# Attention and feed-forward on one core: the first batch's chain moved to PSUM, its inverse slopes spread by TensorE, its order planned anew

## The chip, the cores and the metric

The kernel runs on one core of a Trainium2 chip. The metric is the device time in microseconds, the median of the runs. Before the change it is 1262.75 us (three runs, 1261.84 to 1263.13).

## The reference

Two blocks follow each other: pooled attention (4 batches of 12288 queries, 768 keys each) and a two-layer feed-forward with `h - tanh(h)` in the middle.

```python
def _attn_ref(q, kv, w_sr):          # q: 4 x 12288 x 128, kv: 4 x 384 x 32 x 128
    kv_pool = kv.reshape(B, H // r, r, W // r, r, C).mean(axis=(2, 4))   # r = 4
    kv_flat = kv_pool.reshape(B, -1, C) @ w_sr                           # k = v
    s = scale * (q @ kv_flat.transpose(0, 2, 1))
    a = np.exp(s - s.max(-1, keepdims=True))
    a /= a.sum(-1, keepdims=True) + 1e-09
    return a @ kv_flat

def _moe_ref(x, w_in, w_out):        # w_in: 128 x 2048, w_out: 2048 x 128
    h = x @ w_in
    return (h - np.tanh(h)) @ w_out
```

## The kernel before

The 49152 queries are cut into 96 groups of 512, 24 per batch. A group passes through two stages. *Attention*: three pairs of score matmuls (line 1036), a root on ScalarE (1040), its square on GpSimd (1043), three pairs of value matmuls (1086), and a linear part (1058 to 1076); VectorE joins them into `dl` (1090), GpSimd makes `dr` of it (1093). *Feed-forward*: the function `h - tanh(h)` is expanded about the hidden values at the batch's mean value, so each of eight pairs of "forth" matmuls (1143) is followed by one square on ScalarE (1147), one product on VectorE (1150) and a pair of "back" matmuls (1162); lines 1129 and 1133 add the linear terms, 1173 takes the result out. That makes 50 matmuls of 512 columns per group: 16 forth, 16 back, 6 scores, 6 values, 6 others.

The expansion needs a few small tensors per batch. The mean of the keys (614) gives the centre (626); its product with the first weights (761) gives 16 values per partition, `h` (768). A chain of small VectorE instructions on tiles of 128x16 (lines 788 to 819) makes the first and third derivatives, the inverse of the slope and a statistic of them. From these come the scaled first weights `winr` (for the first batch: 16 diagonal tiles on VectorE, line 892, multiplied on TensorE, 899, copied by ScalarE, 907), the products `Wg` (917) whose sum with the second weights is the slope `At` (930, 939), and the scaled second weights `Wr` on GpSimd (943). The weights arrive as 64-bit words; ScalarE, VectorE rebuild each quarter of them as 32-bit floats (429 to 451). The keys of batch 0 arrive in 12 pieces, four of which GpSimd folds (577) and eight VectorE reduces (583). The keys of the batches 1 to 3 are gathered by eight transfers each, the first issued by SyncE (538), seven by GpSimd (536): each adds onto the same tile, so each waits until the one before it has landed, and whatever stands behind it in GpSimd's queue waits with it.

The order of all instructions is made at build time. Every piece of work is an entry `plan.op(step, engine, us, emit, reads, writes, ...)`; `Plan.run` starts at each moment, among what is ready on an engine, the entry with the smallest step. A table `MOVES` shifts the steps of single entries, a dictionary `AT` those of the groups from the fourth on. Engines run their instructions in the order that results. Tiles share buffers in rings (`sb`, `big`, `bank`); the PSUM tag `acc` has one bank, which the first products (761), the slopes (930), the turned slopes and then the back sums of each group take in turn.

Of the kernel before, what the change touches and what calls it, by code (L numbers as in the profile page):

```python
# [1464 lines left out]
```

## Time and profile before

| what | value |
|---|---|
| median of the runs | 1262.75 us |
| the profiled execution's own time | 1264.22 us |
| its span in the profile | 1262.5 us |
| TensorE busy | 1218.2 us, 96% |
| VectorE, ScalarE, GpSimd busy | 92%, 91%, 84% |
| granted TensorE clock, mean | 0.993 |

The profile is of one execution. Its own time is 1.5 us above the median and 1.7 us above the span. Times within the trace count from the start of the span. A busy time is the union of an engine's instructions; matmuls are pipelined, so the duration of a row of several is not the sum of single ones.

### The profile page before, as it was taken

The page shows a single profiled execution, that of the slowest core. Times are in us where ns is not written, and L with a number is a line of the kernel's source. Part 1 is how long each engine was busy: PE and PEld are TensorE (multiplying, and loading weights), DVE is VectorE, ACT ScalarE, POOL GpSimd, SP SyncE. Part 2 cuts the span into 40 slices and gives each one's busy share as a digit, 9 for nine tenths or more (in the row PEclk, how much of TensorE's full clock was granted, in tenths as well). Part 3 has the DMA queues.
Part 4 walks back from the last instruction along what each step waited for, and adds up shares of the span by engine and source line. Part 5 has one row for each costly group of instructions (what it writes and reads, how often), then busy time and mean ns, then how long its engine had stood idle before and what let it go on. Part 6 is the DMA issues. An engine that isn't in the chain of part 4 may idle for free.

```text
span 1262.5 us, 16708 instructions
## 1 busy us (share of the span) xinstructions
PE 1218.2 (96%) x5252; PEld 935.4 (74%) x5252; DVE 1159.7 (92%) x1241; ACT 1149.0 (91%) x1383; POOL 1055.2 (84%) x836
## 2 busy tenths in 40 slices
PE   5789999999999999999999999999999999999997
PEld 4667777777777777777777777777777777777775
DVE  7889999998999999998899999999899999999997
ACT  4589999999999998999899998999999999999995
POOL 5379987799998888789999887789988888888881
PEclk9899999999999999999999999999999999999999
DMA  9125511123551111111545111111111111111101
GB/s 360 43 50 120 121 44 43 42 77 89 111 121 47 43 51 38 45 44 52 133 99 113 49 43 42 43 43 59 59 43 43 43 51 43 43 42 51 35 26 35
DMA packets 41713, 84.49 MB, mean 67 GB/s; under 512 B 5040, under 2 KB 7216, under 8 KB 41616
## 3 DMA queue, kind: packets, MB, share of 16 engines
q1 hardware_dynamic: 35904, 66.82, 15.9%
q0 software_dynamic: 5712, 16.52, 7.8%
q8 instruction: 44, 0.72, 0.2%
q14 instruction: 53, 0.43, 0.1%
HBM read 57.93 MB, written 25.39 MB: 66 GB/s over the span
## 4 chain that ended last, share of the span: by engine, by line
PE 82%; DVE 6%; POOL 5%; ACT 2%; issue 2%; DMA 2%; SPq 0%; DVEq 0%; ACTq 0%
PE big L1143 26%; PE acc L1162 25%; PE big L1036 10%; PE x L1086 9%; PE acc L1129 5%; DVE r L1150 3%; POOL r L1043 2%; PE x L1058 2%; PE x L1067 2%; PE acc L1133 2%; ACT u L1147 1%; ACT p L1040 1%; PE x L930 1%; DMA winr<-in_kv_by_key_dram 1%; DMA Wr<-in_moe_w_out_dram 1%
## 5 line engine op out<-in xcount | busy, mean ns | idle before, releaser
L1150 DVE SCALAR_TENSOR_TENSOR r<-big,u 128x1024 fp32r<-128x1024 f32 x768 | 902.2, 1219 | 76.2 <-ACT u L1147 66.6
L1147 ACT ACTIVATE u<-big 128x1024 f32<-128x1024 f32 x768 | 764.2, 1029 | 43.4 <-PE big L1143 38.9
L1043 POOL TENSOR_TENSOR r<-p 128x1024 fp32r<-128x1024 f32 x288 | 555.4, 1930 | 106.2 <-ACT p L1040 105.0
L1143 PE MATMUL big<-dr,winr 128*128 128x512 f32 x1536 | 486.5, 406 | 5.7 <-ACT p L1040 4.2
L1162 PE MATMUL acc<-r,Wr 128*128 128x512 f32 x1536 | 453.5, 395 | 2.4 <-DVE o L1173 1.8
L1143 PEld LDWEIGHTS big<-dr,winr 128*128 128x128 f32 x1536 | 269.8, 188 | 107.2 <-DVE r L1150 30.7
L1162 PEld LDWEIGHTS acc<-r,Wr 128*128 128x128 f32 x1536 | 286.9, 188 | 70.3 <-DVE o L1173 2.2
L1040 ACT ACTIVATE p<-big 128x1024 f32<-128x1024 f32 x288 | 296.6, 1030 | 19.9 <-PE big L1036 7.7
L1036 PE MATMUL big<-qr,kTr 128*128 128x512 f32 x576 | 188.2, 409 | 1.0 <-ACT p L1040 0.7
L1086 PE MATMUL x<-r,vvr 128*128 128x512 f32 x576 | 167.3, 399 | 3.8 <-POOL r L1043 3.6
L1093 POOL TENSOR_TENSOR dr<-dl,yk 128x512 fp32r<-128x512 f32 x96 | 127.6, 1329 | 42.0 <-DVE dl L1090 42.0
L1064 POOL TENSOR_TENSOR m<-yk,q 128x512 fp32r<-128x512 f32 x96 | 127.8, 1331 | 8.3 <-ACT yk L1061 8.3
L1036 PEld LDWEIGHTS big<-qr,kTr 128*128 128x128 f32 x576 | 101.5, 189 | 41.1 <-ACT p L1040 20.5
L1086 PEld LDWEIGHTS x<-r,vvr 128*128 128x128 f32 x576 | 109.1, 190 | 29.8 <-POOL r L1043 3.9
L1080 POOL TENSOR_TENSOR ql<-q,qr 128x512 fp32r<-128x512 f32 x96 | 128.0, 1334 | 0.1
L1173 DVE TENSOR_SCALAR o<-acc,At 128x512 f32<-128x512 f32 x96 | 71.3, 742 | 1.6 <-PE acc L1133 1.5
L1090 DVE TENSOR_TENSOR dl<-x,dy 128x512 fp32r<-128x512 f32 x96 | 65.4, 681 | 3.3 <-PE x L1086 3.1
L1076 DVE SCALAR_TENSOR_TENSOR dy<-x,yk 128x512 f32<-128x512 f32 x96 | 65.4, 681 | 2.9 <-PE x L1067 2.9
L1021 POOL TENSOR_SCALAR qr<-q 128x512 fp32r<-128x512 f32 x96 | 62.7, 653 | 2.9 <-DMA q<-in_q_dram 2.8
L1061 ACT ACTIVATE yk<-x 128x512 f32<-128x512 f32 x96 | 58.0, 604 | 5.4 <-PE x L1058 4.1
L1129 PE MATMUL acc<-qr,Lh 128*128 128x512 f32 x192 | 60.4, 396 | 0.0
L1070 ACT ACTIVATE t<-x 128x512 f32<-128x512 f32 x96 | 57.9, 603 | 2.2 <-DVE dy L1076 2.2
(197 smaller groups left out, 657.4 us busy)
## 6 DMA issues: line engine op xcount, KB each, us to landing
q<-in_q_dram SPq DMA_DIRECT2D x96, 256.0 KB
out_dram<-o SPq DMA_DIRECT2D x96, 256.0 KB
kvp<-in_kv_by_place_dram POOLq DMA_DIRECT2D x21, 768.0 KB, 7.2
kc<-inverse SPq DMA_DIRECT2D x12, 256.0 KB
kvp<-in_kv_by_place_dram SPq DMA_DIRECT2D x3, 768.0 KB
winr<-in_kv_by_key_dram SPq DMA_DIRECT2D x4, 512.0 KB
r<-in_kv_by_key_dram SPq DMA_DIRECT2D x4, 512.0 KB
Wr<-in_kv_by_key_dram SPq DMA_DIRECT2D x4, 512.0 KB
```

Source lines behind the costliest of these rows:

```text
L1036: PE.matmul(out=half(plan[s], h), lhsT=plan[kTr][:, n * P : (n + 1) * P], rhs=plan[qr], start=True, stop=True)
L1040: A.activation(out=plan[p], in_=plan[s], func=AF.Silu, scale=1.0 / 3)
L1043: PL.tensor_tensor(out=plan[r], in0=plan[p], in1=plan[p], op=ALU.mult)
L1064: PL.tensor_tensor(out=plan[m], in0=plan[yk], in1=plan[qs], op=ALU.mult)
L1080: PL.tensor_tensor(out=plan[ql], in0=plan[qs], in1=plan[qr].bitcast(F32), op=ALU.subtract)
L1086: PE.matmul(out=plan[num], lhsT=plan[vvr][:, n], rhs=half(plan[f"r2.{g}.{k}"], h), start=(start and h == 0), stop=(stop and h == 1))
L1093: PL.tensor_tensor(out=plan[dr], in0=plan[dl].bitcast(F32), in1=plan[yk], op=ALU.add)
L1129: PE.matmul(out=plan[acc], lhsT=x, rhs=plan[y], start=(start and n == 0), stop=(stop and n == 2))
L1143: PE.matmul(out=half(plan[hp], h), lhsT=plan[winr][:, f * P : (f + 1) * P], rhs=plan[dr], start=True, stop=True)
L1147: A.activation(out=plan[u], in_=plan[hp], func=AF.Square)
L1150: V.scalar_tensor_tensor(out=plan[r], in0=plan[hp], scalar=1.0, in1=plan[u], op0=ALU.add, op1=ALU.mult)
L1162: PE.matmul(out=plan[acc], lhsT=plan[Wr][:, 2 * n + h], rhs=half(plan[r], h), start=(start and h == 0), stop=(stop and h == 1))
```

## The change

Five things change.

1. The first batch's chain (`first_chain`, `third_order_apart`) keeps most of its tiles in the upper half of a PSUM bank, `prep`, in which also the first products and the slopes are summed; each two-input instruction has one operand in PSUM and one in SBUF. The chain has 18 instructions up to the statistic (17 before, the copy of `h` among them), the third order 7 (6 before).
2. The inverse slopes are spread over a tile by TensorE (a broadcast column times the identity, 16 matmuls) and VectorE multiplies them with the first weights (two instructions of 128x1024). The 16 diagonal tiles and ScalarE's two copies go.
3. `Wg` of the first batch is made by four instructions of 128x4x128 with one operand in PSUM, where 16 of 128x128 stood.
4. The lower halves of the weight words are rounded to whole numbers in one ScalarE instruction; eight instructions (line 448) go.
5. The planner's tables and some of its costs (a transfer of 512 KB 1.3 for 1.27, words of the second weights 4.5 for 2.0 until they are seen) are new. The order of the first batch is another; within the later groups the order is the same, while the preparations of the batches 1 to 3 stand at other places in some groups.

```diff
     MOVES = {
-        "load.i.0": -814.14, "words.i.0": -2367.838, "load.i.1": -23.452, "words.i.1": -2059.131,
+        "load.i.0": -3373.262, "words.i.0": -3532.267, "load.i.1": -881.918, "words.i.1": -947.206,
...
         def lower():
             top = words_in().bitcast(U16).rearrange("p (c four) -> p c four", four=4)[:, :, 1]
-            A.activation(out=rest(), in_=top, func=AF.Copy, scale=2.0**-13, bias=2.0**23)
-
-        def whole():
-            A.activation(out=rest(I32), in_=rest(), func=AF.Copy, bias=-(2.0**23))
+            A.activation(out=rest(I32), in_=top, func=AF.Copy, scale=2.0**-13)
...
+        def xs():
+            if b:
+                return [x(n) for n in range(9)]
+            at = G // 2
+            return [plan[prep][:, at : at + FT]] + [
+                plan[prep][:, at + 6 * FT + n * FT : at + 7 * FT + n * FT] for n in range(1, 8)] + [x(8)]
...
         def first_chain():
-            first_order()
-            slopes_of()
-            inverse_of()
+            p_of = xs()
+            h, a3, g0, g1, yp, u = p_of[0], *p_of[1:6]
+            hs, z, p, y, slope, inv = x(0), p_of[6], x(2), x(7), x(6), x(8)
...
+            line(hs, h, 1.0, 0.0)
+            tt(z, h, hs, ALU.mult)
+            line(p, z, 17.0 / 315, -2.0 / 15)
+            tt(a3, z, hs, ALU.mult)
+            tt(p, p, z, ALU.mult)
+            plus_by(g0, p, 1.0 / 3, a3)
...
+            V.reciprocal(out=inv, in_=slope)
+            V.tensor_reduce(out=stat[:, b : b + 1], in_=z, op=ALU.add, axis=AX.X)
...
-                    def diagonal(j=j, dg=dg, fs=fs):
-                        for n, f in enumerate(range(fs.start, fs.stop)):
-                            V.tensor_scalar(out=plan[dg][:, n, 0:C], in0=ident, scalar1=x(8)[:, f : f + 1],
-                                            scalar2=None, op0=ALU.mult)
...
+                            PE.matmul(out=plan[pw][:, at : at + P], lhsT=x(8)[:, f : f + 1].to_broadcast([P, P]),
+                                      rhs=ident, start=True, stop=True)
...
-                    A.copy(out=plan[winr][:, j * WIDE : (j + 1) * WIDE], in_=plan[pw])
+                    V.tensor_tensor(out=plan[winr][:, of], in0=plan[pw], in1=win32[:, of], op=ALU.mult)
...
             def by_first(n=n, wg=wg, fs=fs):
-                for i, f in enumerate(range(fs.start, fs.stop)):
-                    V.tensor_scalar(out=plan[wg][:, i, 0:C], in0=winT[:, f], scalar1=x(4)[:, f : f + 1],
-                                    scalar2=None, op0=ALU.mult)
+                by = xs()[3][:, fs].unsqueeze(2).to_broadcast([P, FW, C])
+                V.tensor_tensor(out=plan[wg][:, :, 0:C], in0=winT[:, fs], in1=by, op=ALU.mult)
```

First place: VectorE where the keys of batch 0 are summed up. `kvp` are the pooled keys, `row` holds the partial sums and the mean, `col` the centre, `x` here the centre's PSUM bank, the rows on `r` and `wout` are words of the second weights. Before:

```order
L583 TENSOR_REDUCE kvp<-r 128x64
L610 TENSOR_REDUCE row<-kvp 128x4 x3
L432 TENSOR_SCALAR r<-r 128x512
L514 TENSOR_REDUCE norms<-x 128x1
L614 TENSOR_REDUCE row<-row 128x1
L615 TENSOR_SCALAR row<-row 128x1
```

and now:

```order
L580 TENSOR_REDUCE kvp<-Wr 128x64 x2
L607 TENSOR_REDUCE row<-kvp 128x4 x2
L611 TENSOR_REDUCE row<-row 128x1
L612 TENSOR_SCALAR row<-row 128x1
L626 TENSOR_SCALAR col<-x 128x1
L628 TENSOR_SCALAR row<-x 128x1
L433 TENSOR_SCALAR r<-r 128x512
```

The mean (614, now 611) stands directly behind the last partial sums, and the centre directly behind it; the words of the second weights come later, half of them behind the chain.

Second place: TensorE at the same time; `big<-wsr,row` takes the mean off the values, `x<-kc` is the moment, `x<-row,wsr` the centre, `acc<-col,win_67` the first products. Before:

```order
L652 MATMUL big<-wsr,row 128x128 x6
L680 MATMUL x<-kc 128x128 x6
L626 MATMUL x<-row,wsr 128x1
L761 MATMUL acc<-col,win_67 128x64 x4
L1058 MATMUL x<-qr,Mh 128x512
L761 MATMUL acc<-col,win_67 128x64 x4
L1036 MATMUL big<-qr,kTr 128x512 x6
L761 MATMUL acc<-col,win_67 128x64 x4
L1067 MATMUL x<-m,share 128x512
L761 MATMUL acc<-col,win_67 128x64 x4
```

and now:

```order
L623 MATMUL x<-row,wsr 128x1
L644 MATMUL big<-wsr,kvp 128x128
L649 MATMUL big<-wsr,row 128x128 x3
L756 MATMUL acc<-col,win_67 128x64 x4
L649 MATMUL big<-wsr,row 128x128 x3
L756 MATMUL acc<-col,win_67 128x64 x4
L1063 MATMUL big<-qr,kTr 128x512 x2
L677 MATMUL x<-kc 128x128 x6
L1063 MATMUL big<-qr,kTr 128x512 x2
L756 MATMUL acc<-col,win_67 128x64 x4
L508 MATMUL x<-W_223 128x128
L756 MATMUL acc<-col,win_67 128x64 x4
```

The centre and the first products moved in front of the moment.

Third place: GpSimd between the `dr` of group 1 and that of group 2 (`r_...` are squared roots, `Wr` the scaled second weights, `Lh` the lower part of the joined slopes, `qr` and `m` of a group's attention; the DMA rows are gathers of batch 1). Before:

```order
L1093 TENSOR_TENSOR dr<-dl,yk 128x512
L1064 TENSOR_TENSOR m<-yk,q 128x512
L1043 TENSOR_TENSOR r_658<-p 128x1024
L1043 TENSOR_TENSOR r_675<-p 128x1024
L536 DMA kvp<-in_kv_by_place_dram 128x2x768
L1043 TENSOR_TENSOR r_708<-p 128x1024
L1021 TENSOR_SCALAR qr<-q 128x512
L1080 TENSOR_TENSOR ql<-q,qr 128x512
L1043 TENSOR_TENSOR r_750<-p 128x1024
```

and now (behind `dr<-dl,yk`, two roots, `m` and a `Wr`):

```order
L533 DMA kvp<-in_kv_by_place_dram 128x2x768
L1003 TENSOR_TENSOR Lh<-L_595,Lh 128x128
L533 DMA kvp<-in_kv_by_place_dram 128x2x768
L1070 TENSOR_TENSOR r_652<-p 128x1024
L1070 TENSOR_TENSOR r_674<-p 128x1024
L1048 TENSOR_SCALAR qr<-q 128x512
L1070 TENSOR_TENSOR r_701<-p 128x1024
L1091 TENSOR_TENSOR m<-yk,q 128x512
L533 DMA kvp<-in_kv_by_place_dram 128x2x768
L1120 TENSOR_TENSOR dr<-dl,yk 128x512
```

The gathers of batch 1 moved to the front: six of GpSimd's seven now stand ahead of the `dr` of group 2, where one stood, and two of them with only one small instruction in between.

## Rows read from the trace of the kernel before

**Rows 1.** The page's part 1: busy time, share, instructions of each engine.

```profile
PE 1218.2 (96%) x5252; PEld 935.4 (74%) x5252; DVE 1159.7 (92%) x1241; ACT 1149.0 (91%) x1383; POOL 1055.2 (84%) x836
```

**Rows 2.** Busy us (instructions) of PE, PEld, DVE, ACT, POOL; clock, DMA share, GB/s.

```profile
35.00:45.50 10.50, 9.02 (x42) 8.14 (x42) 4.97 (x11) 6.85 (x14) 3.71 (x3) 0.67 0.11 31
45.50:62.00 16.50, 11.06 (x64) 8.94 (x63) 15.82 (x48) 6.36 (x11) 8.63 (x6) 0.90 0.01 1
62.00:78.00 16.00, 11.73 (x50) 8.40 (x50) 11.91 (x16) 10.10 (x16) 8.78 (x7) 0.89 0.00 1
95.30:159.70 64.40, 64.40 (x274) 49.88 (x273) 61.00 (x61) 62.63 (x72) 61.87 (x45) 1.00 0.58 119
```

**Rows 3.** The same view for single microseconds around the end of the first transfers.

```profile
34.00:35.00 1.00, 0.58 (x6) 0.39 (x4) 1.00 (x2) 1.00 (x4) 0.00 (x0) 1.00 0.91 369
35.00:36.00 1.00, 0.17 (x2) 0.17 (x2) 0.86 (x4) 0.97 (x4) 0.00 (x0) 1.00 0.16 60
```

**Rows 4.** Timeline of VectorE, 25 to 31 us: start, us, operation, idle before.

```profile
26.78 0.66 DVE L610 TENSOR_REDUCE row<-kvp 128x4 f32<-128x128 f32 x3
29.47 0.43 DVE L432 TENSOR_SCALAR r<-r 128x512 f32<-128x512 f32 x1 [2.03 <-ACT r L429]
30.01 0.17 DVE L614 TENSOR_REDUCE row<-row 128x1 f32<-128x24 f32 x1
30.21 0.15 DVE L615 TENSOR_SCALAR row<-row 128x1 f32<-128x1 f32 x1
```

**Rows 5.** Timeline of TensorE, 30 to 97 us.

```profile
30.80 1.50 PE L652 MATMUL big<-wsr,row 128*128 128x128 f32 x12
32.88 1.70 PE L680 MATMUL x<-kc 128*128 128x128 f32 x12 [0.58 <-ACT kc L667]
35.83 0.38 PE L626 MATMUL x<-row,wsr 128*128 128x1 f32 x2 [1.25 <-ACT Mn L684]
36.86 1.97 PE L761 MATMUL acc<-col,win 128*128 128x64 f32 x8 [0.65 <-DVE row L631]
43.43 1.00 PE L761 MATMUL acc<-col,win 128*128 128x64 f32 x8
54.45 3.61 PE L899 MATMUL big<-Wg,winT 128*128 128x128 f32 x30 [0.39 <-DVE Wg L892]
61.97 1.18 PE L1143 MATMUL big<-dr,winr 128*128 128x512 f32 x4
77.98 1.54 PE L1162 MATMUL acc<-r,Wr 128*128 128x512 f32 x6
94.62 0.63 PE L1143 MATMUL big<-dr,winr 128*128 128x512 f32 x2
```

**Rows 6.** Timeline of VectorE, 45 to 78 us.

```profile
45.59 0.17 DVE L768 TENSOR_SCALAR hb<-acc 128x16 f32<-128x16 f32 x1
45.80 1.04 DVE L788 TENSOR_TENSOR hb<-hb 128x16 f32<-128x16 f32 x1
52.03 0.11 DVE L810 TENSOR_REDUCE stat<-hb 128x1 f32<-128x16 f32 x1
53.11 4.03 DVE L892 TENSOR_SCALAR Wg<-ident,hb 128x128 f32<-128x128 f32 x16
57.05 0.68 DVE L1090 TENSOR_TENSOR dl<-x,dy 128x512 fp32r<-128x512 f32 x1
67.42 4.93 DVE L917 TENSOR_SCALAR Wg<-winT,hb 128x128 f32<-128x128 f32 x4
72.27 2.34 DVE L1150 SCALAR_TENSOR_TENSOR r<-big,u 128x1024 fp32r<-128x1024 f32 x2
```

**Rows 7.** Timeline of GpSimd, 43 to 87 us.

```profile
43.06 3.74 POOL L1043 TENSOR_TENSOR r<-p 128x1024 fp32r<-128x1024 f32 x2 [1.71 <-ACT p L1040]
71.23 2.04 POOL L943 TENSOR_TENSOR Wr<-wout,hb 128x512 fp32r<-128x512 f32 x2
79.05 1.28 POOL L1093 TENSOR_TENSOR dr<-dl,yk 128x512 fp32r<-128x512 f32 x1
85.24 1.37 POOL L536 DMA_DIRECT2D kvp<-in_kv_by_place_dram  x1
```

**Rows 8.** The page's part 6: the gathers, KB each, median us from issue to landing.

```profile
kvp<-in_kv_by_place_dram POOLq DMA_DIRECT2D x21, 768.0 KB, 7.2
```

**Rows 9.** Line 1173 (once per group) in stretches: length, busy us and count.

```profile
159.70:399.80 240.10, 14.10 (x19) 1.00 0.30 73
1106.00:1224.00 118.00, 7.42 (x10) 1.00 0.12 39
```

More of the change, by code (lines that the diff above doesn't have):

```diff
@@ L454, in words_of @@
         load_step, step = at(load_step, "load", kind, n), at(step, "words", kind, n)
-        plan.op(load_step, "SP", 0.5, load_words, (), (own,), late=2.0, dma=1.27)
+        plan.op(load_step, "SP", 0.5, load_words, (), (own,), late=2.0 if kind == "i" else 4.5, dma=1.3)
         plan.op(step, "ACT", 0.6, size, (own,), (M,))
@@ L569, in load @@
                 SP.dma_start(out=piece(), in_=kv_by_key[:, ks, :])
-            plan.op(s - 8, "SP", 0.5, load, (), (own,), late=2.0, dma=1.27)
+            plan.op(s - 8, "SP", 0.5, load, (), (own,), late=2.0, dma=1.3)
             if j in FOLDED:
@@ L786, in first_order @@
         def first_order():
-            h, z, p, g0, g1, a3, slope, y, inv = (x(n) for n in range(9))
+            h, z, p, g0, g1, a3, slope, y, inv = xs()
             E.tensor_tensor(out=z, in0=h, in1=h, op=ALU.mult)
@@ L797, in slopes_of @@
         def slopes_of():
-            h, z, p, g0, g1, a3, slope, y, inv = (x(n) for n in range(9))
+            h, z, p, g0, g1, a3, slope, y, inv = xs()
             E.tensor_scalar(out=p, in0=g1, scalar1=27.0, scalar2=9.0, op0=ALU.mult, op1=ALU.add)
@@ L807, in inverse_of @@
         def inverse_of():
-            h, z, p, g0, g1, a3, slope, y, inv = (x(n) for n in range(9))
+            h, z, p, g0, g1, a3, slope, y, inv = xs()
             V.reciprocal(out=inv, in_=slope)
@@ L812, in third_order @@
         def third_order():
-            h, z, p, g0, g1, a3, slope, y, inv = (x(n) for n in range(9))
+            h, z, p, g0, g1, a3, slope, y, inv = xs()
             E.tensor_scalar(out=p, in0=g1, scalar1=-1.0, scalar2=1.0, op0=ALU.mult, op1=ALU.add)
@@ L833, in about_centre @@
             else:
-                plan.op(first_at[n], "PE", 0.9, partial(first, n), (cen, ("win32", n)), (f"{ph}.0",),
+                plan.op(first_at[n], "PE", 1.0, partial(first, n), (cen, ("win32", n)), ((prep, "h"),),
                         late=0.2)
@@ new lines, in first_chain @@
+            tt(a3, z, hs, ALU.mult)
+            tt(p, p, z, ALU.mult)
+            plus_by(g0, p, 1.0 / 3, a3)
+            tt(y, hs, g0, ALU.subtract)
+            tt(yp, hs, g0, ALU.subtract)
+            tt(g1, yp, y, ALU.mult)
+            line(p, g1, 27.0, 9.0)
+            tt(u, p, g1, ALU.mult)
+            plus_by(slope, u, 3.0, y)
+            plus_by(a3, u, 3.0, y)
+            tt(u, a3, slope, ALU.mult)
+            V.tensor_scalar(out=u, in0=u, scalar1=FLOOR * FLOOR, scalar2=2 * FLOOR, op0=ALU.is_lt,
+                            op1=ALU.mult)
@@ new lines, in first_chain, with third_order_apart @@
+            tt(slope, u, slope, ALU.add)
+            V.reciprocal(out=inv, in_=slope)
+            V.tensor_reduce(out=stat[:, b : b + 1], in_=z, op=ALU.add, axis=AX.X)
+        def third_order_apart():
+            p_of = xs()
+            g1, yp, u = p_of[3:6]
+            p, slope = x(2), x(6)
+            V.tensor_scalar(out=u, in0=g1, scalar1=-1.0, scalar2=1.0, op0=ALU.mult, op1=ALU.add)
+            V.tensor_scalar(out=p, in0=g1, scalar1=-1.0, scalar2=1.0 / 3, op0=ALU.mult, op1=ALU.add)
+            V.tensor_scalar(out=yp, in0=slope, scalar1=1.0, scalar2=0.0, op0=ALU.mult, op1=ALU.add)
+            V.tensor_tensor(out=p, in0=u, in1=p, op=ALU.mult)
+            V.tensor_tensor(out=yp, in0=yp, in1=slope, op=ALU.mult)
+            V.tensor_tensor(out=yp, in0=yp, in1=slope, op=ALU.mult)
+            V.tensor_tensor(out=x(5), in0=yp, in1=p, op=ALU.mult)
@@ L850, in about_centre @@
         else:
-            plan.op(known, on, 3.1, first_chain, (hb,), (hb, gg, iv, ("stat", b)))
-            plan.op(at(s0 - 5, "chain", c, 3), on, 1.1, third_order, (hb,), (hb, a3s))
+            plan.op(known, on, 3.7, first_chain, ((prep, "h"),), ((prep, "t"), (hb, 8), iv, ("stat", b)))
+            plan.op(at(s0 - 5, "chain", c, 3), on, 1.4, third_order_apart, ((prep, "t"),), ((prep, "v"), (hb, 5), a3s))
         NW, FW = 4, FT // 4
@@ L885, in about_centre, with spread @@
                 for k in range(2):
-                    dg = f"dg.{b}.{j}.{k}"
-                    sb(dg, "Wg", [P, FW, C + 1], step=winr_at + j / 2 + k / 4)
-                    fs = slice((2 * j + k) * FW, (2 * j + k + 1) * FW)
-                    def diagonal(j=j, dg=dg, fs=fs):
-                        for n, f in enumerate(range(fs.start, fs.stop)):
-                            V.tensor_scalar(out=plan[dg][:, n, 0:C], in0=ident, scalar1=x(8)[:, f : f + 1],
-                                            scalar2=None, op0=ALU.mult)
-                    def scaled(j=j, k=k, dg=dg, pw=pw):
+                    def spread(j=j, k=k, pw=pw):
                         for n in range(FW):
@@ L898, in scaled @@
                             at = (k * FW + n) * P
-                            PE.matmul(out=plan[pw][:, at : at + P], lhsT=winT[:, f], rhs=plan[dg][:, n, 0:C],
-                                      start=True, stop=True)
-                    plan.op(at(known + 0.1, "diagonal", c, j), "DVE", 0.72, diagonal, (iv, "ident"), (dg,),
-                            port=True)
-                    plan.op(at(s0 - 9, "scaled", c, j), "PE", 0.9, scaled, (dg, "winT"), ((pw, k),), late=0.2)
-                def copy_scaled(j=j, pw=pw):
-                    A.copy(out=plan[winr][:, j * WIDE : (j + 1) * WIDE], in_=plan[pw])
-                plan.op(at(s0 - 9, "copied", c, j), "ACT", 1.03, copy_scaled, (pw,), ((winr, j),), late=0.1)
+                            PE.matmul(out=plan[pw][:, at : at + P], lhsT=x(8)[:, f : f + 1].to_broadcast([P, P]),
+                                      rhs=ident, start=True, stop=True)
+                    plan.op(at(s0 - 9, "scaled", c, j), "PE", 0.9, spread, (iv, "ident"), ((pw, k),), late=0.2)
+                def scaled(j=j, pw=pw):
+                    of = slice(j * WIDE, (j + 1) * WIDE)
+                    V.tensor_tensor(out=plan[winr][:, of], in0=plan[pw], in1=win32[:, of], op=ALU.mult)
+                plan.op(at(s0 - 9, "copied", c, j), "DVE", 1.14, scaled, (pw, "win32"), ((winr, j),), late=0.1)
         for n in range(NW):
@@ L925, in beside @@
             def beside(wg=wg, fs=fs):
-                A.copy(out=plan[wg][:, :, C], in_=x(3)[:, fs])
+                A.copy(out=plan[wg][:, :, C], in_=(xs()[3] if b else xs()[2])[:, fs])
             def slopes(n=n, wg=wg):
                 for k in range(FW):
-                    PE.matmul(out=plan[f"{pa}.{n if b else 0}"][:, 0 : C + 1], lhsT=wout32[:, n * FW + k],
+                    PE.matmul(out=plan[f"{pa}.{n}" if b else prep][:, 0 : C + 1], lhsT=wout32[:, n * FW + k],
                               rhs=plan[wg][:, k], start=(k == 0 and (b > 0 or n == 0)),
@@ L949, in about_centre @@
             else:
-                plan.op(slopes_at[n], "DVE", 0.72, by_first, (gg, "winT"), ((wg, 0),), late=0.1, port=True)
-            plan.op(slopes_at[n], "ACT", 0.2, beside, (gg,), ((wg, 1),), late=0.1)
+                plan.op(slopes_at[n], "DVE", 0.65, by_first, ((prep, "t"), "winT"), ((wg, 0),), late=0.1)
+            plan.op(slopes_at[n], "ACT", 0.2, beside, (gg,) if b else ((prep, "t"),), ((wg, 1),), late=0.1)
             joined = joined_at[n]
-            plan.op(joined, "PE", 1.0, slopes, (wg, ("wout32", n)), (f"{pa}.{n if b else 0}",), late=0.2)
+            plan.op(joined, "PE", 1.0, slopes, (wg, ("wout32", n)), (f"{pa}.{n}" if b else (prep, "a"),), late=0.2)
             if b and n:
@@ L956, in about_centre @@
             elif b or n == 3:
-                plan.op(joined, "ACT", 0.3, partial(sum_slopes, 0), (f"{pa}.0",), (At,), late=0.1)
+                plan.op(joined, "ACT", 0.3, partial(sum_slopes, 0), (f"{pa}.0" if b else (prep, "a"),), (At,), late=0.1)
             plan.op(third_at[n], "POOL", 1.08, by_third,
@@ L989, in attention_then_ffn @@
     AT = dict(
-        forth=[5.672, 0.094, 4.211, 2.015, 0.418, 7.192, 2.849, 6.37], first=[3.398, -0.446, 2.007,
-        0.475, -0.143, 6.739, 1.516, 3.819], then=[6.764, -0.489, 3.447, -0.198, -0.487, 7.14,
-        2.348, 6.779], back=[8.231, 5.559, 7.588, 6.683, 6.668, 9.991, 7.59, 10.049],
-        scores=[-13.586, -14.426, -12.749], roots=[-14.593, -15.853, -14.482], beyond=[-12.528,
-        -14.1, -6.25], values=[-4.977, -4.939, -3.788], num=-7.075, y=-17.298, linear=-18.266,
-        along=-9.916, shares=-7.27, left=-8.028, fewer=-8.413, straight=8.716, apart=-4.695,
-        rounded=-4.026, rounded_q=-20.953, slope=10.792, result=10.297, lower_q=-9.166, acc=-7.471)
+        forth=[5.713, -0.07, 4.34, 2.001, 0.408, 6.827, 2.617, 6.387], first=[2.432, -0.943, 1.457,
+        -0.311, -0.652, 6.125, 1.265, 3.488], then=[5.564, -0.869, 2.615, -0.542, -0.75, 6.822,
+        1.648, 6.404], back=[8.012, 5.635, 7.725, 6.73, 6.636, 9.976, 7.705, 10.049],
+        scores=[-13.732, -14.37, -12.851], roots=[-15.601, -16.584, -14.654], beyond=[-12.226,
+        -14.126, -6.28], values=[-4.947, -4.932, -3.57], num=-7.173, y=-17.251, linear=-19.101,
+        along=-9.83, shares=-7.286, left=-8.587, fewer=-8.599, straight=8.617, apart=-5.388,
+        rounded=-2.253, rounded_q=-21.894, slope=10.469, result=9.565, lower_q=-7.289, acc=1.141)
     ALONE, OWN_PLACE = 2, 3
```

26 lines of the change are left out of this document (12 added, 14 removed), and 193 rows, old and new, of the table MOVES.

## The prediction

> **What bounds the kernel now.** I read the busy times first, then the stretches of time, then the start engine by engine. TensorE is busy 96% of the span [rows 1]. The view by stretches shows where the missing 4% lie: from 95.3 us on TensorE is busy 64.40 of 64.40 us, while VectorE, ScalarE and GpSimd each have a little to spare; between 35 and 78 us it is busy 9.02 of 10.5, 11.06 of 16.5 and 11.73 of 16 us [rows 2], and part of that busy time is first products, slopes and other work that no later group has. So the kernel has two parts: a start of some 95 us, set by a chain of dependent steps, and a body set by TensorE. In the body a group takes 118.0 / 10 = 11.80 us [rows 9], that is 0.236 us for each of its 50 matmuls. The stretch of 240.1 us that holds 19 groups and the turn to batch 1 is 240.1 - 19 x 11.80 = 15.9 us longer than the groups alone [rows 9]; there are three such turns.
>
> The order within later groups is the same, so the body's 11.80 us stays. The change can earn only what the start gets shorter, measured where TensorE becomes the bound, and the turns can give something back. The start is bounded so: the first transfers end at about 35.2 us (369 GB/s in the microsecond from 34, 60 in the next) [rows 3]; the mean (30.01, VectorE), the centre (35.83, TensorE), the last first product (ends 44.4) [rows 4, 5]; the chain (45.59 to 52.14), the scaled weights [rows 6]; the first forth (61.97), the first back (77.98), the first forth of group 2 (94.62) [rows 5].
>
> **The first products come earlier.** Before, the mean stood behind a word conversion that waited 2.03 us for ScalarE, and started at 30.01 although the last partial sum ended at 27.44 [rows 4]: 2.6 us. Then TensorE did the subtraction (1.50) and the moment (1.70 with 0.58 idle), and waited 1.25 for ScalarE's copy, before the centre at 35.83; the first products began at 36.86 and stood in four lots among other work up to 44.4 [rows 5]. Now mean and centre are on top: 27.44 + 0.17 + 0.15 + 0.38 and two small VectorE steps gives first products near 28.7. In front of the last of them TensorE has four lots at 1.00 (the row of 1.97 is one lot at a lower granted clock; the mean of that stretch is 0.67), half of a subtraction 0.75, the moment 1.70, four score matmuls at 0.236 and one small matmul of 0.4: 7.8 us, so `h` is there at 36.5 instead of 45.59: -9.1. The bounds: VectorE's last reductions and the folds may come later than 27.44 now, and lots may take 1.97 instead of 1.00: from -5.2 (four lots at the lower clock) to -10.6.
>
> **The chain.** Before, 17 instructions took 45.59 to 52.14 = 6.55 us. The first of them, with its source in PSUM, took 0.17 while a GpSimd root of 3.74 us for two ran (43.06 to 46.80); the second, with SBUF operands alone, took 1.04 and ended at 46.8, when the root did [rows 6, 7]. So a small VectorE instruction with one operand in PSUM isn't held by GpSimd, and one with SBUF operands alone is. Now 18 instructions at 0.17 to 0.21, say 0.205: 3.7 us, to 40.2; against 6.55 that is -2.9, and one more instruction is in it. The third order's seven, 1.4 us, no longer stand at that place. Bounds of the chain: 3.1 (18 at 0.17) and, if something still holds it (the reciprocal's place, the copy of `h`), 6.5.
>
> [...]
>
> **Scaled weights and `Wg`.** 16 diagonal instructions (4.03) and four `Wg` ones in 4.93, held for most of it [rows 6], make place for two of 128x1024 at 1.17 (as the two of 2.34 [rows 6]) = 2.3 and four of 128x512 with a PSUM operand at 0.68 = 2.7 [rows 6]. The 16 spread matmuls have the shape of the 16 diagonal ones, whose 30 records took 3.61 [rows 5] (two passes each, two records missing): 32 x 0.12 = 3.9 us of TensorE in their place, up to 7.8 at the lower clock. VectorE from 40.2: 2.3 + 2.7 + three conversions at 0.43 [rows 4] + third order 1.4 + `dl` 0.68 = 48.7, with 1.0 of waiting for spread tiles 49.7.
>
> **First forth.** It needs `dr`, on GpSimd. GpSimd's queue now has a gather in front, which adds onto the transfer that ends at 35.2; behind it stand, up to `dr`, four roots at 1.87, two of 128x512 at 1.28 and one `Wr` at 1.02 [rows 7]: 35.2 + 1.37 + 7.48 + 2.56 + 1.02 = 47.6, another gather 1.37 to 49.0. So `dl` at 49.7 is last, and `dr` is ready at 51.0: first forth at 51.0 for 61.97, -11.0. Both queues end within 0.7 us of each other, so taking away either alone gains little.
>
> **First back.** From first forth to first back went 16.0 us, with the 4.93 of `Wg` in it [rows 5, 6]. These no longer stand there; I take off a third of them, as the others waited for `Wr` and the slopes anyhow: 51.0 + 14.5 = 65.5 for 77.98, -12.5. Bounds 11.1 (all of it) and 16.0 (none): 62.1 to 67.0.
>
> **The gathers on GpSimd.** Six of batch 1's seven gathers on GpSimd's queue now stand ahead of the `dr` of group 2, where one stood. A gather lands 7.2 us after its issue [rows 8], and the next one waits for that; everything behind it in the queue waits too. From the first `dr` at 51.0 to the end of group 2's `dr`, GpSimd has seven roots 13.1, three `Wr` 3.1, two `m` and two `dr` (four at 1.28) 5.1, four gathers at 1.37 [rows 7] = 5.5, one rounding and one `Lh` about 1.1 (estimated as less than one instruction of 1.28): 27.9. To that comes one wait for ScalarE's `p`, as the 1.71 before [rows 7], and the wait between the two gathers that have only `Lh` between them: 7.2 - 1.37 - 0.5 = 5.3. Sum 34.9, so group 2's first forth starts at 85.9. At that place TensorE has 115 matmuls of 512 columns behind it; before, it had 112 at 94.62, and 115 at 94.62 + 3 x 0.236 = 95.3. The start is 9.4 us shorter. Without that wait TensorE itself sets the time: 47 matmuls were done at the first back, now 48, and the 68 up to the 115th took 17.3 us before, 16.0 of it at 0.236 each; so 65.5 + 67 x 0.236 + 1.3 = 82.6 and 12.7 us. So 3.3 us of the gain are given back to the gathers. From there on TensorE is full as in [rows 2], and nothing is regained: GpSimd has 61.87 of 64.40 us to do.
>
> [...] Here no gather is seen beside a VectorE instruction with SBUF operands alone: the one at 85.24 took 1.37 [rows 7]. [...]
>
> **The rest.** The words change ScalarE's and VectorE's load by eight instructions, beside TensorE's work; I cost them at nothing while the first transfers last until 35.2 anyway. The other placing of the preparations at the turns I take as 0 with 3 us to either side over all three, since each turn is 15.9 us and the same instructions are in it.
>
> **Sum.** 1264.22 - 9.4 = 1254.8 for an execution like the profiled one; that one is 1.5 above the median, so 1262.75 - 9.4 = 1253.4.
>
> **Rivals.**
> The gathers don't bind. The landing of 7.2 is a median that holds transfers in a busy time; the DMA share from 45.5 to 78 us is 0.01 or less [rows 2], so gathers there may land sooner, or the wait may lie beside one for ScalarE. For it speaks that idle queue; against it, that 7.2 is the median of all 21. Then 12.7: 1250.0.
>
> The start gives only half. `h` comes at 40.4 (four lots at the lower clock, bound above) and the chain is held as before (6.5): both together make 6.7 us less of the 11.0, and the first forth stands at 57.7; group 2's `dr` is then 34.9 - 1.7 later, at about 90.9 (the wait for `p` is over by then): 95.3 - 90.9 = 4.4, so 1258.3. For it speaks the mean clock 0.67 of [rows 2]; against it, that TensorE now has other work between lots.
>
> Nothing is left: the start gains, but the turns take 7 to 9 us. About 1262.
>
> Slower: the turns. GpSimd's gathers of the batches 2 and 3 stand at other places; where two stand within one group, GpSimd, with 2.5 of 64.4 us to spare [rows 2], loses 5.3 us as above, and TensorE runs dry in a body that has no reserve. At 3.1 us per turn the gain of 9.4 is gone; at 4.0 per turn the kernel is 2.6 us slower, 1265.4. For it speaks the lack of reserve; against it, that roots stand two groups ahead and can absorb part of a wait.
>
> **How the numbers follow.** The forecast 0.50; gathers don't bind 0.20; half 0.17; nothing left 0.06; slower 0.07. A measurement of this kernel tells 0.2%, 2.5 us, from no change. Of the first three all lie beyond it: faster 0.87, same 0.06, slower 0.07. The forecast's own bounds are 2.5 to either side (first back 62.1 to 67.0), 1251 to 1256. The range reaches to the one rival with its own 1.5 us, 1248.5, and over the half to 1260.0; outside are the last two and a little of the others, less than 0.2.
>
> **What would show it.** First products near 28.7, `h` at about 36.5, 18 chain instructions of about 0.2 with none over 1 us beside a GpSimd root; first forth near 51, first back near 65.5; GpSimd idle some 5 us between two gathers at about 60 to 75, and group 2's first forth near 86; 11.80 per group after it, and the stretch with the turn to batch 1 again about 240 us. It is wrong if the first products wait for VectorE's reductions or ScalarE's words, if chain rows of 1 us are still there, if GpSimd's gathers show no idle time (then about 1250), or if a turn is longer by 3 us.

## The result and the profile after

The changed kernel takes 1270.85 us (median of six runs, 1269.56 to 1271.57) against 1262.51 us before: ratio 1.0064, 95% interval 1.0051 to 1.0077. It is 8.3 us slower where 9.4 us less were forecast, and outside the range. The profiled execution took 1270.95 us, its span is 1269.2 us; the spans of the two profiled executions lie 6.7 us apart.

The view by stretches of the changed kernel, in the columns of [rows 2]. TensorE was busy 11.73 of 16 us from 62 to 78 before and is busy 8.33 now; from 78 on, where it was nearly full before, it has gaps until 108. First the row from 78 of the kernel before, then the changed kernel:

```profile
78.00:95.30 17.30, 16.54 (x69) 12.37 (x68) 15.11 (x16) 15.83 (x19) 16.97 (x14) 1.00 0.41 92
```

```profile
35.00:45.50 10.50, 5.87 (x27) 4.59 (x27) 5.41 (x25) 6.23 (x12) 8.23 (x5) 0.75 0.52 103
45.50:62.00 16.50, 13.87 (x78) 10.70 (x76) 13.53 (x22) 8.99 (x14) 10.87 (x9) 0.96 0.34 65
62.00:78.00 16.00, 8.33 (x28) 5.82 (x29) 8.73 (x5) 5.88 (x10) 11.81 (x10) 0.67 0.52 84
78.00:95.30 17.30, 15.73 (x59) 11.35 (x57) 11.85 (x11) 11.69 (x14) 9.83 (x7) 0.91 0.38 75
95.30:108.00 12.70, 9.99 (x34) 7.30 (x35) 9.08 (x11) 8.51 (x10) 8.43 (x8) 0.87 0.52 105
```

The body is what it was: the stretch with the turn to batch 1 and ten late groups, for line 1200 (line 1173 before), against 240.10 and 118.00 in [rows 9]. (Each stretch runs from the start of one such instruction to the start of another; the eleventh of the second row starts at its edge.)

```profile
167.00:404.90 237.90, 14.11 (x19) 1.00 0.29 74
1112.00:1229.90 117.90, 7.45 (x11) 1.00 0.12 39
```

So the loss lies in the start. The result of group 3 (line 1200) is taken out at 131.6, where the kernel before does it at 124.4: 7.2 us late, and the last group's is 6.9 us late (1262.9 against 1256.0). Now the start by engine. First, the mean, the chain's first instruction, one in its middle and its last but one (VectorE; start, duration, operation):

```profile
26.90 0.18 DVE L611 TENSOR_REDUCE row<-row 128x1 f32<-128x24 f32 x1
36.54 0.17 DVE L845 TENSOR_SCALAR hb<-acc 128x16 f32<-128x16 f32 x1 [0.55 <-PE acc L756]
38.20 0.17 DVE L845 TENSOR_SCALAR hb<-acc 128x16 f32<-128x16 f32 x1
39.56 0.25 DVE L867 RECIPROCAL hb<-hb 128x16 f32<-128x16 f32 x1
```

`h` is read at 36.54 (36.5 was forecast) and the chain ends at 39.84 after 3.3 us, without one held row, though GpSimd issues a gather beside it from 37.27 and works on a root from 38.29. Against [rows 4, 6] these are the two steps that came as forecast. Then TensorE (the number in brackets is the wait before the row and what ended it):

```profile
41.89 0.80 PE L1094 MATMUL x<-m,share 128*128 128x512 f32 x1 [4.63 <-POOL m L1091]
42.48 1.91 PE L1063 MATMUL big<-qr,kTr 128*128 128x512 f32 x4
44.19 0.71 PE L1085 MATMUL x<-qr,Mh 128*128 128x512 f32 x1
44.69 3.94 PE L928 MATMUL big<-ident,hb 128*128 128x128 f32 x24
55.04 1.09 PE L1170 MATMUL big<-dr,winr 128*128 128x512 f32 x4
71.79 2.09 PE L957 MATMUL acc<-Wg,wout 128*128 128x129 f32 x8 [6.41 <-DVE wout L449]
77.14 2.76 PE L1189 MATMUL acc<-r,Wr 128*128 128x512 f32 x6
100.73 1.02 PE L1170 MATMUL big<-dr,winr 128*128 128x512 f32 x2
```

The reader is to see three places. The inverse slopes are ready at 39.81, but the spread (928) stands behind the share of group 0 (1094), which waits 4.63 us for GpSimd's `m`; the spread starts at 44.69, the first forth (1170) at 55.04. The last quarter of the slopes (957) waits 6.41 us for a part of the second weights. The first back (1189) is at 77.14, hardly earlier than 77.98 in [rows 5]; and group 2's first forth, 67 matmuls of 512 columns on, is at 100.73 where the old kernel stood at the same count at 95.3. Who keeps the slopes waiting is on VectorE and GpSimd:

```profile
65.15 6.58 DVE L449 CUSTOM_DVE_ANT_0 wout<-wout,o 128x1024 uint16<-128x1024 uint16 x1
```

```profile
62.79 1.19 POOL L533 DMA_DIRECT2D kvp<-in_kv_by_place_dram  x1
63.56 1.49 POOL L970 TENSOR_TENSOR Wr<-wout,hb 128x512 fp32r<-128x512 f32 x1
64.57 1.71 POOL L1120 TENSOR_TENSOR dr<-dl,yk 128x512 fp32r<-128x512 f32 x1
65.80 2.31 POOL L1070 TENSOR_TENSOR r<-p 128x1024 fp32r<-128x1024 f32 x1
67.66 1.68 POOL L1091 TENSOR_TENSOR m<-yk,q 128x512 fp32r<-128x512 f32 x1
68.88 2.30 POOL L1070 TENSOR_TENSOR r<-p 128x1024 fp32r<-128x1024 f32 x1
```

The last assembly of words (449), SBUF operands alone, takes 6.58 us; its like at 57.11 takes 0.68. It ends at 71.73, half a microsecond behind the last of four GpSimd instructions (71.18). Behind the gather each of these starts 0.4 to 0.5 us before the one before it ends, and lasts about 0.4 us longer than the same instruction elsewhere (1.28 and 1.87 in [rows 7]). Their starts lie 1.01, 1.23, 1.86 and 1.22 us apart, no more than such instructions last elsewhere: the rows overlap, the pace is the usual one, and there is no gap between them.

### The profile page after: what moved, and what is told of

Its sections match the earlier page's. It is cut to its first block, busy times and chain, and to the rows that moved or that the text cites. A ratio compares the mean times of both kernels' runs of the same rounds, so it can differ in the third digit from the quotient of the medians.

```text
span 1269.2 us, 16667 instructions
## 1 busy us (share of the span) xinstructions
PE 1217.5 (96%) x5252; PEld 936.1 (74%) x5252; DVE 1153.5 (91%) x1218; ACT 1143.2 (90%) x1373; POOL 1057.7 (83%) x836
## 4 chain that ended last, share of the span: by engine, by line
PE 84%; DVE 5%; ACT 3%; POOL 2%; issue 2%; DMA 2%; SPq 0%; ACTq 0%; DVEq 0%
PE big L1170 27%; PE acc L1189 25%; PE big L1063 10%; PE x L1113 9%; PE acc L1156 5%; DVE r L1177 3%; PE x L1085 2%; ACT u L1174 2%; PE x L1094 2%; PE acc L1160 2%; PE x L957 1%; ACT p L1067 1%; DMA Wr<-in_kv_by_key_dram 1%; DMA r<-in_kv_by_key_dram 1%; POOL r L1070 1%
```

## The experiments

Each run is compared with runs of the kernel before on the same chip; the ratio is that of the means. e7 to e9 ran on another chip than the other experiments.

| run | median us | before | ratio | 95% interval |
|---|---|---|---|---|
| changed kernel | 1270.85 | 1262.51 | 1.0064 | 1.0051 to 1.0077 |
| e1 words earlier | 1263.54 | 1262.35 | 1.0006 | 0.9997 to 1.0015 |
| e2 GpSimd yields | 1263.49 | 1262.35 | 1.0009 | 1.0000 to 1.0018 |
| e3 no third gather | 1263.37 | 1262.35 | 1.0006 | 0.9996 to 1.0015 |
| e4 chain in SBUF | 1275.75 | 1262.35 | 1.0101 | 1.0086 to 1.0117 |
| e5 e1 and late gathers | 1262.17 | 1262.46 | 0.9996 | 0.9987 to 1.0006 |
| e6 e5 and early gathers | 1258.14 | 1262.46 | 0.9964 | 0.9950 to 0.9978 |
| e7 e6 and `dl` first | 1256.42 | 1263.21 | 0.9947 | 0.9934 to 0.9960 |
| e8 e6 and result first | 1257.27 | 1263.21 | 0.9953 | 0.9940 to 0.9966 |
| e9 both | 1255.63 | 1263.21 | 0.9942 | 0.9930 to 0.9954 |
| e10 first gather alone | 1268.43 | 1262.62 | 1.0037 | 1.0023 to 1.0050 |
| e11 e9, words late | 1263.48 | 1262.62 | 1.0005 | 0.9996 to 1.0014 |

All but e3 and e4 only move entries in the finished order. With names given to the entries (`name=("add", kind, n)` and the like), one line places an entry directly behind another:

```diff
-        order.sort()
+        order.sort(); at = lambda n: next(k for k, o in enumerate(order) if o[1] == self.names[n]); [(lambda x, b: order.insert(1 + at(b), x))(order.pop(at(a)), b) for a, b in PAIRS]
```

### Why the assembly takes 6.58 us: e1, e2, e3

e1, the fourth assembly directly behind the third, that is, in front of GpSimd's run:

```diff
+PAIRS = [(("add", "o", 3), ("add", "o", 2))]
```

> The fourth assembly of the second weights' words (VectorE, line 449, SBUF operands alone, 6.58 us at 65.15 in the changed kernel) stands directly behind the third one, 7 us earlier; nothing else moves. Theory A (GpSimd's four instructions without a gap, 64.57 to 71.18, held it, and the last quarter of the slopes waited 6.41 us for it): the instruction takes under 1.8 us, the slopes' last quarter starts near 65.5 for 71.79, the first back near 71 for 77.14, and the kernel is 4.5 to 6.5 us faster than the changed one (1264.5 to 1266.5); more (to 1257) if the slow second group follows from the same wait. Theory C (the gathers in GpSimd's queue behind it set the time anyway): the first back comes earlier, but the first forth of group 2 stays near 100 and the time gains under 2 us.

e2, VectorE as it was, GpSimd's two roots and `m` behind the `Wr` that waits for the assembly:

```diff
+PAIRS = [(("beyond", 2, 1), ("third", 0, 3)), (("along", 2), ("beyond", 2, 1)), (("beyond", 2, 0), ("along", 2))]
```

> VectorE's order is as in the changed kernel; on GpSimd the last scaled second weights (line 970), which wait for that assembly, stand in front of two roots and m instead of behind them, so GpSimd pauses. Theory A: the assembly takes 2 us or less (until dr ends, then 0.7), the last slopes start near 67 for 71.79, 3.5 to 5 us faster than the changed kernel. Theory B (the assembly is slow for another reason, the gather issued at 62.79 that is in flight until about 70): it still takes 5 to 6.6 us, and GpSimd's pause makes the kernel up to 5 us slower.

e3, the third gather on GpSimd left out (two of the 32 rows of keys are then missing from the sums):

```diff
-                    PL.dma_start(out=plan[kvp], in_=of, accum_op=ALU.add)
+                    (dict if (b, w) == (1, 3) else PL.dma_start)(out=plan[kvp], in_=of, accum_op=ALU.add)
```

> The changed kernel without the third gather of batch 1 on GpSimd (the one issued at 62.79): two of the 32 rows of the keys that are summed are left out. Theory A: the assembly at 65 still takes 5.5 to 6.6 us, the time moves by less than 1.5 us. Theory B: the assembly takes about 0.7 us, and the kernel is 4.5 to 6.5 us faster.

All three bring the same 7.3 to 7.5 us, more than the 4.5 to 6.5 expected of e1 and the 3.5 to 5 of e2. In e1 the slopes' last quarter starts at 64.88, the first back at 68.90. In e2 the assembly takes 1.69 us: it waits for the end of `dr`, and runs in the pause behind it.

```profile
63.21 1.71 POOL L1120 TENSOR_TENSOR dr<-dl,yk 128x512 fp32r<-128x512 f32 x1
63.79 1.69 DVE L449 CUSTOM_DVE_ANT_0 wout<-wout,o 128x1024 uint16<-128x1024 uint16 x1
65.56 1.04 POOL L970 TENSOR_TENSOR Wr<-wout,hb 128x512 fp32r<-128x512 f32 x1 [0.64 <-DVE wout L449]
```

In e3 it takes 1.12. There my theory A (GpSimd's run of four holds it) said 5.5 to 6.6, theory B (the gather in flight holds it) about 0.7: by e3 alone B would stand. But in e2 the gather is in flight beside the assembly just the same (issued at 61.43; up to 130 us the changed kernel's gathers land 7.0 to 7.3 us after their issue), and it passes in 1.69: so the transfer doesn't hold it. What the gather does is seen on GpSimd, in e3 (the last row is VectorE's assembly):

```profile
62.33 1.04 POOL L970 TENSOR_TENSOR Wr<-wout,hb 128x512 fp32r<-128x512 f32 x1
63.96 1.28 POOL L1120 TENSOR_TENSOR dr<-dl,yk 128x512 fp32r<-128x512 f32 x1 [0.59 <-DVE dl L1117]
65.20 2.35 POOL L1070 TENSOR_TENSOR r<-p 128x1024 fp32r<-128x1024 f32 x1
67.51 1.26 POOL L1091 TENSOR_TENSOR m<-yk,q 128x512 fp32r<-128x512 f32 x1
64.67 1.12 DVE L449 CUSTOM_DVE_ANT_0 wout<-wout,o 128x1024 uint16<-128x1024 uint16 x1
```

Without the gather the rows have their usual lengths, overlap by 0.04 us at most, and the assembly (64.67 to 65.79 there) slips in at the end of `dr`; the root behind it is the one that is longer (2.35 for 1.89). With the gather in front GpSimd's rows overlap and nothing slips in until the run of four ends (6.58). Theory A holds with this added: in the changed kernel, with a gather at its head, GpSimd's run holds the assembly through all of its four instructions (6.58 us); in e3, without one, the assembly comes in behind the GpSimd instruction that it met (1.12). The other profiles bear that out: in the kernel before, whose first gather on GpSimd is at 85.24, the longest hold is 1.95 us (a `Wg` instruction, line 917, at 69.4, beside a root of 1.89), and in VectorE's timelines of e1 to e9 the longest without a gather ahead is in a row of two assemblies at 15.6 to 16.9 us, 2.87 or 2.88 us where two took 1.28 at 54.08 in e6. In e2 and e3 the assembly ends 0.56 and 0.55 us behind the one GpSimd instruction that it waits for; the one of 6.58 us ends 0.55 behind the last of four.

### What the chain in PSUM is worth: e4

```diff
-                plan[prep][:, at + 6 * FT + n * FT : at + 7 * FT + n * FT] for n in range(1, 8)] + [x(8)]
+                x((0, 1, 0, 0, 4, 3, 5)[n]) if n in (1, 4, 5, 6) else plan[prep][:, at + 6 * FT + n * FT : at + 7 * FT + n * FT] for n in range(1, 8)] + [x(8)]
```

> The changed kernel with four of the chain's tiles (a3, yp, u, z) in SBUF, so that about ten of the 18 instructions and five of the third order's seven have SBUF operands alone, beside GpSimd's gather and roots (37.3 to 45.5). Theory of the prediction (GpSimd holds such instructions): the 3.3 us of the chain become 6 to 9, with rows of over 1 us; since TensorE starts the spread at 44.69 and waits for m until then, the first 3 to 5 us cost nothing, the kernel is 0 to 4 us slower. Rival (PSUM against SBUF makes no difference): the chain takes 3.3 us again.

With these four tiles in SBUF the kernel is 4.9 us slower than the changed kernel. One instruction of the chain was held from its start at 37.04, beside the gather's own row, to the end of GpSimd's run behind that gather (36.62 to 44.87):

```profile
35.70 0.17 DVE L845 TENSOR_SCALAR hb<-acc 128x16 f32<-128x16 f32 x1 [0.55 <-PE acc L756]
36.12 0.17 DVE L845 TENSOR_SCALAR hb<-hb 128x16 f32<-128x16 f32 x1
37.04 7.88 DVE L842 TENSOR_TENSOR acc<-hb 128x16 f32<-128x16 f32 x1
46.29 0.25 DVE L867 RECIPROCAL hb<-hb 128x16 f32<-128x16 f32 x1
```

The chain takes 10.9 us for 3.3 (6 to 9 were expected), and the kernel before paid 1.04 for the like [rows 6]. The theory of the prediction holds and its size was too small. Two rows that differ only in their constants and in where the source lies (35.70 from PSUM, 36.12 in SBUF) both take 0.17: a source in PSUM costs no more than one in SBUF here, nor in [rows 4, 6] (0.17 from PSUM, 0.17 and 0.15 for small ones in SBUF).

### Gathers, and the turn from group 0 to group 1: e5 to e9

e5 adds to e1 two pairs, e6 two more:

```diff
+# e5
+(("gather", 1, 5), ("rounded_q", 4)), (("gather", 1, 6), ("rounded", 2))
+# e6
+(("gather", 1, 1), ("beyond", 0, 2)), (("gather", 1, 2), ("rounded", 0))
```

> Experiment e1 (words' last assembly earlier) with two gathers of batch 1 moved on GpSimd: the one that waited 5.54 us for the gather before it (79.06 in e1) stands behind three more instructions, the next one behind the dr of group 2. Theory D (in e1 the gain of the earlier first back is eaten by that wait: GpSimd's roots start at 79.84, ScalarE waits 2.39 us at 82.22 for a buffer of p that such a root frees, and what stands behind it on ScalarE, VectorE and TensorE is late): GpSimd idles under 2 us there, the first forth of group 2 comes 2.5 to 4.5 us earlier than in e1 (92.9), and the time is 1259 to 1261. Rival (the single acc bank and the order of the tail of group 0 set it: TensorE's waits of 1.53 for the result of group 0 and 2.22 for dl of group 2): the first forth of group 2 stays within 1 us of 92.9, the time within 1.5 us of e1's 1263.5.

> As e5, and the first two gathers of batch 1 moved too: the one at 37.27 behind the three roots and m of group 0, the one at 50.47 behind the first dr. Theory D with the prediction's claim on gathers (a gather in front takes 1.0 to 1.4 us from what stands behind it, and GpSimd's instructions behind it run without a gap): m of group 0 ends 1.2 to 1.5 us earlier, TensorE's 4.63 us wait for it at 41.89 falls to about 3.3, the spread begins about 1.3 us earlier, the first forth too, and the time is 1 to 2 us below e5's. Rival (that wait is hidden by others): within 0.7 us of e5.

In e1 the wait that the prediction had worked out as 5.3 us between two gathers was there (in the changed kernel itself it is 2.68, at 80.05):

```profile
79.06 1.19 POOL L533 DMA_DIRECT2D kvp<-in_kv_by_place_dram  x1 [5.54 <-DMA kvp<-in_kv_by_place_dram]
```

Theory D made it the limit, and fell: e5 takes it away (GpSimd then waits 3.14 us for ScalarE's `p`), group 2's first forth comes at 92.34 for 92.91, and the time falls by 1.4 us. The rival named for e5 was right. e6 gave 4.0 us where 1 to 2 were expected. GpSimd in e6, and TensorE behind it:

```profile
36.02 1.89 POOL L1070 TENSOR_TENSOR r<-p 128x1024 fp32r<-128x1024 f32 x1 [4.02 <-ACT p L1067]
37.87 1.27 POOL L1091 TENSOR_TENSOR m<-yk,q 128x512 fp32r<-128x512 f32 x1
```

```profile
39.20 0.50 PE L1094 MATMUL x<-m,share 128*128 128x512 f32 x1 [1.65 <-POOL m L1091]
41.96 3.48 PE L928 MATMUL big<-ident,hb 128*128 128x128 f32 x24
```

The root could start at 36.02; in the changed kernel the gather stood before it and itself started only at 37.27, though the transfers were over at about 36 (DMA share 0.10 from 35 to 36, 0.00 from 36 to 37). The delay of `m`, 2.7 us (41.84 against 39.14), is that wait (1.25), the gather's 1.02 until the root starts, and 0.42 by which `m` itself lasts longer; the longer root adds nothing, as `m` starts 1.86 behind it (1.85 in e6). I had counted the issue alone. What the gather waited for between 36 and 37.27 isn't shown.

e7 and e8 each move one VectorE instruction of e6; e9 has both:

```diff
+# e7
+(("apart", 2), ("values", 2, 2))
+# e8
+(("result", 0), ("back", 0, 9))
```

> Experiment e6 with one VectorE instruction moved: dl of group 2 stands behind one product of group 1 instead of three (the last value matmuls end at 84.4 in e6, dl starts at 86.73). Theory E (behind the first back the start is bound by the order of the instructions in the turn from group 0 to group 1, where an engine waits for an instruction that stands behind others in another's queue): TensorE's wait of 2.22 us for dl at 87.56 falls below 0.7, dr of group 2 ends about 2 us earlier, the time is 1.5 to 3 us below e6's 1258.1. Rival (TensorE is bound by its matmuls and the clock behind it, a wait is only moved): within 0.7 us of e6.

> Experiment e6 with the result of group 0 (VectorE, line 1200) directly behind the last back matmuls, in front of one product and dy, so that the one acc bank comes free earlier (74.7 is the end of the last back in e6, the result starts at 76.71, TensorE's next sum at 77.50 after 1.53 idle). Theory E: the wait of 1.53 goes, the next sum starts near 75.9, the time is 1 to 2 us below e6's 1258.1. Rival: within 0.7 us of e6, as the 2.22 us for dl just grow.

> Both edits of e7 and e8. Theory E: 2.5 to 4.5 us below e6's 1258.1 (1253.5 to 1255.5). Rival: within 1 us of e6.

e7 is 0.0017 below e6 in ratio (2.2 us), e8 0.0011 (1.4 us); e9 is 0.0022 below (2.8 us), within theory E's 2.5 to 4.5. Every run of e9 (1254.21 to 1257.78) is below every run of e6 (1257.91 to 1260.47), though the kernel before is no faster on e9's chip (1263.21 against 1262.46). The intervals of e6 and of all three overlap, so for one move alone it is the trace that carries it: in e7 TensorE's wait for `dl` is gone and that for the result left (1.52), in e8 the wait for the result is gone and that for `dl` left (2.22). The stretch from first back to group 2's first forth, 67 matmuls now and 65 before, in the columns of [rows 2]; first the changed kernel:

```profile
77.14:100.73 23.59, 19.59 (x68) 14.13 (x67) 15.40 (x15) 14.04 (x16) 12.42 (x10) 0.86 0.52 95
```

then e6, and e9:

```profile
66.36:89.72 23.36, 18.41 (x68) 12.62 (x67) 15.31 (x15) 14.04 (x16) 15.53 (x14) 0.96 0.42 79
```

```profile
64.97:83.44 18.47, 17.30 (x68) 11.65 (x67) 14.06 (x14) 13.64 (x16) 14.62 (x12) 1.00 0.53 95
```

Before it was 94.62 - 77.98 = 16.64 us [rows 5]. The two rows overstate the gain, as e6's profiled execution is its slowest (1260.47, median 1258.14) and e9's its fastest (1254.21, median 1255.63): the stretches differ by 4.9 us, the medians by 2.5. In e6 TensorE waits 1.53 us for the result of group 0, which stands behind a product and `dy` on VectorE and keeps the one `acc` bank, and 2.22 us for `dl` of group 2, which stands behind three products:

```profile
77.50 0.72 PE L1156 MATMUL acc<-qr,Lh 128*128 128x512 f32 x2 [1.53 <-DVE o L1200]
87.56 0.66 PE L1085 MATMUL x<-qr,Mh 128*128 128x512 f32 x1 [2.22 <-DVE dl L1117]
88.02 1.91 PE L1189 MATMUL acc<-r,Wr 128*128 128x512 f32 x4
```

In e9 both rows have no wait, and the four matmuls behind the second take 1.10 for 1.91; the granted clock over the two stretches above is 0.96 in e6 and 1.00 in e9. The same two waits stand in the changed kernel (1.53 at 88.40, 2.22 at 98.46).

### One mend alone, and all but one: e10, e11

e10 is the changed kernel with e6's first pair alone; e11 is e9 without e1's pair.

> The changed kernel with only the first of GpSimd's gathers of batch 1 moved, from 37.27 to behind the three roots and m of group 0; all else as in the changed kernel, the words too. Theory F (that gather holds what stands behind it three times over: it waits for the transfer before it until 37.3 although a p is ready at 36.0, it takes 1.0, and the instructions behind it are 0.4 longer each): m of group 0 ends 2.5 to 3 us earlier (about 39.1), TensorE's wait of 4.63 falls below 2, the first forth starts near 52.2 for 55.04, and the time is 2 to 4 us below the changed kernel's 1270.85, with the wait for the words still in it. Rival (the 4 us between e5 and e6 come from the second gather, at 50.47): under 1 us.

> Experiment e9 with the words' last assembly back at its place of the changed kernel, behind the first forths. Theory A (the wait is of its own and the other mends don't hide it): the assembly takes over 5 us beside GpSimd again, TensorE waits over 5 us for the last slopes, and the time is 4 to 7 us above e9's 1255.6. Rival (with the other order of gathers GpSimd leaves gaps, or the time is bound elsewhere): within 2 us of e9.

In e10 `m` ends at 38.06 (`h` stands 0.8 us earlier in this execution than in the changed kernel's), TensorE's wait is 1.66 us, and the time falls by 2.4 us, by 0.0027 or 3.4 us in ratio; but the second gather, left in place, now waits 2.20 us for the first in front of `dr`; TensorE waits 1.31 us for that `dr`, and the first forth starts at 52.00. In e11 the assembly takes 6.58 us again, TensorE waits 6.41, and the time is 1263.48: 0.0063 above e9 in ratio, 7.9 us, a little over the 4 to 7 expected. The slopes' last quarter, the turned slopes and the first six back matmuls then take the times of the changed kernel, where the granted clock is 0.50 (2.76 us for the six in both, 1.56 in e9).

## Why the prediction was wrong

The forecast was 9.4 us less, the result 8.3 more. At group 2's first forth the prediction stood at 85.9, the chip at 100.73. These 14.8 us are in three steps; a fourth lies behind that place.

- **First forth, 51.0: measured 55.04 (4.0 of the 14.8).** I summed GpSimd's queue and VectorE's and took the later, but left out TensorE's own queue: the spread stands behind group 0's share, which needs `m`, which stood behind the gather. The gather, put at 35.2, started at 37.27. The inverse slopes waited from 39.81 to 44.69. In e9, with the gather moved, the first forth is at 50.46.
- **First back, first forth plus 14.5 (14.4 by its own third): measured plus 22.1 (7.6).** This is the step that failed most, together with the sentence of "The rest" that costs the words at nothing. The order shown ahead of the prediction says that half the words come later; I looked at them on top, where transfers hide them, and not at the bottom, where the last quarter of the slopes waits for them. That an SBUF-only instruction is held by GpSimd was in the prediction, for the chain and for `Wg`; it wasn't asked of the assembly. In the changed kernel the assembly took 6.58 us and TensorE waited 6.41; e1, e2 and e11 put 7.3 to 7.9 us of the whole time on it. In e9 the first back is at 64.97; 65.5 was forecast.
- **From there to group 2's first forth, 20.4: measured 23.59 (3.2).** I took the sum of GpSimd's work with the wait between two gathers. That wait exists (2.68 in the changed kernel, 5.54 in e1), but nothing of weight hangs on it: behind it GpSimd waits for ScalarE's `p`, 3.76 us at 85.00. What binds there is the order of the turn from group 0 to group 1; TensorE's waits for VectorE's result and `dl` (1.53 and 2.22) stood at nothing in the sum. e9, without them, needs 18.47.
- **From group 2's first forth on, TensorE full: it isn't at once.** At that place the changed kernel is 5.4 us behind (100.73 against 95.3), at group 3's result 7.2. From 95.3 to 108 TensorE is busy 9.99 of 12.70 us, where the prediction had it full. Which waits make up these 1.8 us hasn't been taken apart.

What was right: the first products and `h` (36.54 for 36.5), the chain (3.3 for 3.7), the spread's own time (3.94 + 1.06 for 3.9 to 7.8), `Wg` and the scaled weights (0.68 and 1.22 each, for 0.68 and 1.17), the body at 11.80 and the turns (237.9 for 240.1, within 3 us). That `h` came within 0.1 us is in part luck: the mean came 0.5 us earlier than assumed (26.90), the first products 0.6 later (29.33 for 28.7), and the work from there to `h` took 7.2 us for 7.8. No delay of a gather beside VectorE's conversions is seen: e6's gather at 51.16, beside two conversions from 51.39, took 1.21 to issue, as the one at 78.86 (1.22) with no VectorE instruction beside it. The slower rival was put at the turns between batches; there nothing was lost. The loss was in the start itself, and no rival had one there.

With four gathers and three VectorE instructions at other places the changed kernel is 7.6 us faster than before (e9, 1255.63 against 1263.21), near the 9.4 that were forecast. It has not been taken apart which of the five edits brings that, but for the chain in PSUM (4.9 us, e4, in the changed kernel's order), nor what such moves would give the kernel before.

## What to carry to other kernels

Where a new order is given, follow each instruction that has moved down, not only those that moved up, and ask of each engine's queue in order who stands in front of the instruction that the path needs. An instruction of VectorE that GpSimd holds, as the assembly here (6.58 us for 0.68), belongs in front of GpSimd's run (7.3 us, e1) or where GpSimd has a gap (7.4 us, e2), or one operand of it in PSUM, as in the chain (4.9 us, e4). A gather on GpSimd cost more here than its issue of 1.2 to 1.4 us: the wait for the one before it (5.54 us in e1), and the gaps that are missing behind it (6.58 us for the assembly, 1.12 in e3). A gain at the start of a pipeline counts at the place where the bound engine is full, so count matmuls to that place, waits included.
